# Two of four batches of the first chunk moved to the path of the later chunks, in a linear attention with a feed-forward layer behind it

## The chip, the cores and the metric

The kernel runs on one core of a Trainium2 chip. The metric is device time in microseconds (us) of one execution; lower is better. A core has five engines with a queue each: TensorE (PE in the rows; PEld is its weight load), VectorE (DVE), ScalarE (ACT), GpSimd (POOL) and SyncE (SP, which here only issues DMAs). An engine works through its queue in order and waits where an instruction's inputs are not there yet.

## The reference

Inputs `r`, `k`, `v`, `w` have the shape (4 batches, 8 heads, 768 steps, 48), `u` is (8, 48). Per batch and head a state of 48 x 48 is carried over the steps:

```python
cur   = outer(u * k_t, v_t)
y_t   = r_t @ (state + cur)
state = w_t[:, None] * state + outer(k_t, v_t)
```

The result, rearranged to 3072 tokens of 384, goes through a feed-forward layer: `h = relu(x @ w_in)` with 384 x 2048 weights, then `(h * h) @ w_out`. All is fp32 at the outside.

## The kernel before, in words

**Tiling.** The 768 steps are cut into 6 chunks of 128. A unit is one chunk of one batch (24 units). Inside a unit the recurrence becomes matrix products: a running product of `w` over the chunk (VectorE scans, line 538), keys and receptances scaled by it and its inverse (lines 545 to 566), scores, a mask, and the product with `v`; the state is carried from chunk to chunk. The `u` term stands on the diagonal of the scores: a bonus sum beta per step and head, the sum over 48 of r, u and k.

**The two paths of a unit.** Chunk 0 (there is no state yet) has a path of its own: inputs are turned by TensorE (line 521), scores (line 760), the mix with `v` (lines 784, 801), keys turned back (line 776) and state sums (line 794) are separate pieces of TensorE, with a hop to ScalarE or VectorE between them. Its bonus sums are a VectorE product (line 554), four matmuls (line 579) and a ScalarE copy (line 585). Units of chunks 1 to 5 go through a staged path instead: keys are turned (line 639), and one block of TensorE holds the mix of one unit together with the scores and state products of the next (lines 672, 681, 654, 691). Its bonus sums are two GpSimd products over the untransposed inputs (lines 588, 590), a VectorE reduction (line 593) and three small VectorE operations that move halves (lines 596 to 598). Its output is written in four banks (lines 615, 618), one of which is spread over the others by six small DMAs (line 729), and the four banks are cleared by ScalarE (line 826). In chunk 0 the output needs no such DMAs.

**The feed-forward layer.** It runs for each chunk over 16 slices f of the 2048, with fp32 values split in a leading and a remaining part. The first layer is nine matmuls (line 864), then ScalarE and VectorE make the square and its two parts (lines 869 to 876; line 876 is the last of them and is VectorE's), and the second layer is three matmuls per batch (line 882). In chunk 0 the slices f = 0 to 5 are done for batches 0 and 1 first (256 columns), and then for batches 2 and 3; from f = 6 on all four go together (512 columns). So chunk 0 has 12 half slices and 10 full ones.

**Weights.** They arrive as 16 blocks and are split once, while chunk 0 runs: a ScalarE pass (line 430), three VectorE passes (lines 434, 438, 443), a ScalarE pass (line 450) and two GpSimd subtractions of 384 columns each (line 452).

**What sets the order.** The program is a list of steps (`P.add(engine, cost, rank, function, r=..., w=...)`); the table ORDER gives the order in which they are issued, PLACES the buffer of each, and FILLS puts idle transposes (line 352) into TensorE's queue where a gap is planned. Each engine runs its steps in that order.

## Time and profile before

| | |
|---|---|
| median of 3 runs | 521.7 us (520.2 to 523.99) |
| the profiled execution | 519.77 us, its span 518.1 us |
| TensorE busy | 503.7 us, 97% of the span |
| VectorE, ScalarE, GpSimd busy | 364.5, 318.6 and 102.7 us |
| granted TensorE clock | 0.998 of 2.4 GHz over the span |
| moved by DMA | 48.73 MB |

A row of the timeline gives the start, the duration, the engine, the line, the operation and the tiles (out <- in), and in brackets the idle time before it and what ended it. Times are from the start of the span. Durations of neighbouring rows overlap a little, since an instruction starts before the one ahead of it has quite ended.

### The profile page before, as it was taken

How to read it: one execution, taken by the hardware profiler on the slowest of the kernel's cores; microseconds unless marked ns; L12 is line 12 of the kernel's file. 1: busy time of each engine (PE TensorE's matmuls, PEld its weight loads, DVE VectorE, ACT ScalarE, POOL GpSimd, SP SyncE). 2: the span in 40 equal slices, each digit the busy share in tenths (PEclk: the TensorE clock that was granted, in tenths of full speed). 3: DMA queues.
4: the chain of work that ended last, by engine and by line, in shares of the span. 5: the costliest groups of instructions: out<-in, count | busy, mean ns of one | idle time of the engine just before them, and what ended most of it. 6: DMA issues, size and time to landing. Idle time of an engine off the chain costs nothing.

```text
span 518.1 us, 13748 instructions
## 1 busy us (share of the span) xinstructions
PE 503.7 (97%) x5432; PEld 457.2 (88%) x5432; DVE 364.5 (70%) x799; ACT 318.6 (61%) x870; POOL 102.7 (20%) x157
## 2 busy tenths in 40 slices
PE   8989899998999999999999999999999999999996
PEld 7879888888999999988899889899888888998895
DVE  6999899999788888759886667678376364333232
ACT  4989889988856767667566375564544353423232
POOL 2134942646021041210402101303000000000000
PEclk9999999999999999999999999999999999999999
DMA  8999998246547565565661572771181000100001
GB/s 162 213 223 184 245 207 179 55 112 105 112 76 124 106 92 110 104 105 85 100 139 32 95 116 44 116 126 28 36 130 32 3 19 6 58 16 1 1 0 65
DMA packets 188311, 48.73 MB, mean 94 GB/s; under 512 B 178001, under 2 KB 183122, under 8 KB 188242
## 3 DMA queue, kind: packets, MB, share of 16 engines
q1 hardware_dynamic: 187664, 47.01, 47.8%
q8 instruction: 44, 0.72, 0.6%
q10 hardware_dynamic: 578, 0.79, 0.4%
q14 instruction: 25, 0.20, 0.1%
HBM read 31.66 MB, written 4.72 MB: 70 GB/s over the span
## 4 chain that ended last, share of the span: by engine, by line
PE 79%; DVE 8%; ACT 4%; DMA 4%; issue 2%; SPq 2%; POOL 0%; ACTq 0%; DVEq 0%; POOLq 0%
PE hp L864 34%; PE ob L882 34%; PE ob L672 2%; PE ob L691 2%; PE a L681 2%; DMA st<-in_r_dram 2%; PE a L654 1%; DMA ri<-in_moe_w_in_dram 1%; PE hp L639 1%; DVE q L438 1%; ACT m L634 1%; DVE g L876 1%; SPq L507 1%; DVE q L443 1%; DMA st<-in_k_dram 1%
## 5 line engine op out<-in xcount | busy, mean ns | idle before, releaser
L882 PE MATMUL ob<-wo,g 128*128 128x384 f32 x1152 | 226.7, 339 | 1.4 <-DVE g L876 1.4
L864 PE MATMUL hp<-x,wi 128*128 128x512 f32 (+1 forms) x1062 | 221.9, 354 | 2.4 <-DVE g L876 2.0
L882 PEld LDWEIGHTS ob<-wo,g 128*128 128x128 f32 x1152 | 199.6, 188 | 9.5 <-DVE g L876 1.7
L864 PEld LDWEIGHTS hp<-x,wi 128*128 128x128 f32 x1062 | 174.5, 188 | 28.6 <-DVE g L876 3.5
L869 ACT ACTIVATE t<-hp 128x512 f32<-128x512 f32 (+1 forms) x118 | 60.9, 518 | 81.1 <-PE hp L864 47.1
L873 DVE SCALAR_TENSOR_TENSOR hp<-hp,t 128x512 f32<-128x512 f32 (+1 forms) x96 | 58.1, 606 | 69.3 <-ACT t L869 68.9
L876 DVE TENSOR_TENSOR g<-hp,g 128x512 fp32r<-128x512 f32 (+1 forms) x118 | 69.1, 587 | 39.6 <-ACT g L875 38.7
L875 ACT CAST g<-hp 128x512 fp32r<-128x512 f32 (+1 forms) x118 | 59.5, 505 | 43.0 <-DVE hp L873 42.4
L662 POOL MEMSET S<- 1x1 f32 x20 | 1.8, 88 | 237.3 <-PE ob L672 237.2
L634 ACT ACTIVATE m<-diag,beta 128x64 f32<-128x64 f32 x160 | 40.4, 337 | 1.2 <-DVE beta L597 1.1
L618 DVE SCALAR_TENSOR_TENSOR x<-ob,x 112x128 fp32r<-112x128 f32 x80 | 21.3, 284 | 17.9 <-ACT x L615 14.8
L826 ACT COPY ob<-zero 112x128 f32<-112x128 f32 x80 | 20.7, 268 | 19.4 <-DVE x L618 10.0
L615 ACT ACTIVATE x<-ob 112x128 fp32r<-112x128 f32 x80 | 19.2, 278 | 18.4 <-PE ob L691 14.8
L452 POOL TENSOR_TENSOR wi<-q,wi 128x384 fp32r<-128x384 f32 x16 | 20.8, 1320 | 37.7 <-ACT wi L450 37.7
L538 DVE TENSOR_TENSOR_SCAN pt<-pt,zero 112x128 f32<-112x128 f32 x64 | 24.5, 421 | 3.7 <-DMA pt<-st 2.4
L588 POOL TENSOR_TENSOR st<-st 128x384 f32<-128x384 f32 x20 | 21.0, 1050 | 26.6 <-DMA v<-in_v_dram 15.9
L590 POOL TENSOR_TENSOR st<-st,un 128x384 f32<-128x384 f32 x20 | 23.1, 1160 | 1.0
L452 POOL TENSOR_TENSOR wo<-q,wo 128x384 fp32r<-128x384 f32 x16 | 17.0, 1080 | 30.5 <-ACT wo L450 30.5
L483 DVE STREAM_TRANSPOSE st<-st 128x1152 f32<-128x1152 f32 x16 | 21.5, 1359 | 0.3 <-ACT st L609 0.3
L562 DVE TENSOR_TENSOR pt<-pt,m 112x512 f32<-112x512 f32 x24 | 18.9, 787 | 0.5 <-ACT Ec L561 0.2
L556 DVE TENSOR_TENSOR pt<-pt 112x508 f32<-112x508 f32 x24 | 18.5, 770 | 0.1
L563 DVE SCALAR_TENSOR_TENSOR m<-pt,m 112x512 f32<-112x512 f32 x24 | 17.8, 742 | 0.3
(121 smaller groups left out, 541.0 us busy)
## 6 DMA issues: line engine op xcount, KB each, us to landing
pt<-st SPq DMA_DIRECT2D x96, 96.0 KB, 3.1
ro<-in_moe_w_out_dram SPq DMA_DIRECT2D x8, 768.0 KB, 7.7
v<-in_v_dram SPq DMA_DIRECT2D x96, 48.0 KB, 3.1
out_dram<-q SPq DMA_DIRECT2D x20, 192.0 KB, 2.1
ri<-in_moe_w_in_dram SPq DMA_DIRECT2D x32, 96.0 KB, 5.1
ri<-in_moe_w_in_dram SPq DMA_DIRECT2D x8, 384.0 KB, 6.2
st<-in_k_dram SPq DMA_DIRECT2D x8, 384.0 KB, 4.6
st<-in_w_dram SPq DMA_DIRECT2D x8, 384.0 KB
```

What stands on the lines that cost most here:

```text
L452: P.add("pool", 1.0, rank(8 * k + 5), lambda q=q, tt=tt, z=z: G.tensor_tensor(out=tt[:, 1, z * 384:z * 384 + 384], in0=q.tile[:, z * 384:z ...
L483: V.transpose(out=zt[:, i].rearrange("a t p q i -> a t (p q) i"), in_=sv[:, :, i].rearrange("s t p q x -> s t (p q) x"))
L538: lambda p=p: V.tensor_tensor_scan(out=pt[:, 0, p], data0=src(0)[:, p], data1=zero.broadcast_to([HP, C]), initial=1.0, op0=ALU.mult, op1=A ...
L590: P.add("pool", 0.97, rank("ru"), lambda: G.tensor_tensor(out=rk(), in0=rk(), in1=un.rearrange("s (h d) -> s h d", d=D), op=ALU.mult), r=[ ...
L618: made.append(P.add("dve", c2, rank(nm + "l"), lambda y=y, hi=hi, lo=lo: V.scalar_tensor_tensor(out=lo(), in0=y(), scalar=-1.0, in1=hi().b ...
L634: A.activation(M.tile[:, o:o + Q], diag2, AF.Copy, scale=beta.tile[:, i:i + 1])
L864: T.matmul(hp.tile[:, 0:n], wi[f][:, wl, kt], xT[:, kt, xl, xs], start=(m == 0), stop=(m == 3 * KT - 1))
L869: P.add("act", 0.49 if full else 0.28, rank("g1"), lambda: A.activation(t(), h(), AF.Relu), r=[hp], w=[(g, 1)])
L873: P.add("dve", 0.605 if full else 0.337, rank("g2"), lambda: V.scalar_tensor_tensor(out=h(), in0=h(), scalar=0.0, in1=t(), op0=ALU.max, op ...
L875: P.add("act", 0.48 if full else 0.26, rank("g3"), lambda: A.copy(out=hi(), in_=h()), r=[hp], w=[(g, 0)])
L876: P.add("dve", 0.605 if full else 0.335, rank("g4"), lambda: V.tensor_tensor(out=lo(), in0=h(), in1=hi().bitcast(F32), op=ALU.subtract), r ...
L882: T.matmul(obs[b][:, 0:DM], g.tile[0][:, gl, o:o + C], wo[f][:, wl], start=(f == 0 and m == 0), stop=(f == NF - 1 and m == 2))
```

## The change

Batches 2 and 3 of chunk 0 take the staged path of the later chunks: a new flag `first` (chunk 0 and batch below 2) stands where `c == 0` stood, so the old path serves batches 0 and 1 alone. The two units become the first two stages, their bonus sums go to GpSimd and VectorE, and their outputs go through the four banks, the six DMAs and the clearing. The two GpSimd subtractions per weight block become one of 768 columns. The tables ORDER, PLACES and FILLS are new throughout (they are left out below). No other arithmetic changes.

```diff
-            for z in range(2):
-                P.add("pool", 1.0, rank(8 * k + 5), lambda ...: G.tensor_tensor(out=tt[:, 1, z * 384:z * 384 + 384], ..., op=ALU.subtract),
-                      r=[q, lead], w=[(nm, g, "rest", z)])
+            P.add("pool", 1.9, rank(8 * k + 5), lambda q=q, tt=tt: G.tensor_tensor(out=tt[:, 1], in0=q.tile, in1=tt[:, 0].bitcast(F32), op=ALU.subtract),
+                  r=[q, lead], w=[(nm, g, "rest")])
...
+        first = c == 0 and b < 2
...
-        vt = Slot("v", 4 * c + b) if c else Slot("v0")
+        vt = Slot("v0") if first else Slot("v", 4 * c + b)
...
-            home = (["o0", "o1", "o2"], ["o3", "hp", "hp"], ["o0", "o1", "o2"], ["o3", "a", "o2"])[b] if c == 0 else ["hp"] * 3
+            home = (["o0", "o1", "o2"], ["o3", "hp", "hp"])[b] if first else ["o2", "o3", "hp"] if (c, b) == (0, 2) else ["hp"] * 3
...
-                if c and i in COPIED:
+                if not first and i in COPIED:
...
-        summed = c == 0
+        summed = first
...
-        if c:
+        if not first:
             M, Kt, kp = Ms[0], Slot("m", unit), Slot("hp")
...
-            if (c, b) == (1, 0):
+            if (c, b) == (0, 2):
                 clear(rank)
...
     for i in range(2 * B):
         attention(i // B, i % B, lambda nm, i=i: RANKS.unit(i // B, i % B, nm))
+        if i in (2, 3):
+            advance(stages[0] if i == 3 else None, stages[i - 2])
+        if i == 3:
+            advance(stages[1], None)
...
-            a, z = (stages[k] if 0 <= k < len(stages) else None for k in (i - B - 1, i - B))
+            a, z = (stages[k] if 0 <= k < len(stages) else None for k in (i - 3 if i > B else -1, i - 2))
             advance(a, z)
```

How the tables move the work is seen at three places. The first is VectorE, just ahead of the last write of batch 1's input to the feed-forward layer (line 618 on x0; pt0 holds batches 0 and 1 of chunk 0, pt1 batches 2 and 3, q0 and q1 weights that are being split). Before:

```order
L443 SCALAR_TENSOR_TENSOR q0_155<-ri0_56,q0_155 128x768
L554 TENSOR_TENSOR m2_164<-pt1_136,ob2_149 112x2x4x64
L556 TENSOR_TENSOR pt1_136<-pt1_136 112x4x127
L538 SCALAR_TENSOR_TENSOR pt1_136<-ob3_150,zero_126 112x128
L562 TENSOR_TENSOR pt1_136<-pt1_136,m4_166 112x512
L563 SCALAR_TENSOR_TENSOR m4_166<-pt1_136,m4_166 112x512
L538 SCALAR_TENSOR_TENSOR pt1_136<-ob3_150,zero_126 112x128
L618 SCALAR_TENSOR_TENSOR x0_142<-a0_153,x0_142 128x128
L618 SCALAR_TENSOR_TENSOR x0_142<-a1_154,x0_142 128x2x128
```

And with the change:

```order
L434 TENSOR_SCALAR q1_156<-q1_156 128x768
L593 TENSOR_REDUCE beta3_179<-st01_144 128x8
L438 SCALAR_TENSOR_TENSOR q1_156<-ri0_56,q1_156 128x768
L562 TENSOR_TENSOR pt1_136<-pt1_136,m5_167 112x512
L443 SCALAR_TENSOR_TENSOR q1_156<-ri0_56,q1_156 128x768
L563 SCALAR_TENSOR_TENSOR m5_167<-pt1_136,m5_167 112x512
L434 TENSOR_SCALAR q0_155<-q0_155 128x768
L566 TENSOR_TENSOR pt1_136<-pt1_136,m5_167 112x2x4x64
L618 SCALAR_TENSOR_TENSOR x0_142<-a1_154,x0_142 128x2x128
L618 SCALAR_TENSOR_TENSOR x0_142<-a0_153,x0_142 128x128
```

Batches 2 and 3 are now worked off further before batch 1's output, their reductions (line 593) among it, and the first weight block of the first layer (ri0) is split later.

The second place is TensorE, around the first first-layer product (line 864). Before:

```order
L579 MATMUL ob0_147<-ut_235,m2_164 128x4 x4
L352 MATMUL ob1_148<-ident_116 128x128 x13
L794 MATMUL a1_154<-v01_92,m0_162 64x48
...
L864 MATMUL hp1_152<-x0_142,wi0_57 128x256 x9
L521 MATMUL a1_154<-ident_116,st01_144 112x128 x4
L352 MATMUL ob0_147<-ident_116 128x128 x12
L760 MATMUL a0_153<-pt1_136 64x128
```

And with the change:

```order
L639 MATMUL hp1_152<-ident_116,pt1_136 128x112 x4
L352 MATMUL ob3_150<-ident_116 128x128 x12
L639 MATMUL hp0_151<-ident_116,pt1_136 128x112 x4
L794 MATMUL a1_154<-v01_92,m3_165 64x48
...
L864 MATMUL hp1_152<-x0_142,wi0_57 128x256 x9
L352 MATMUL ob3_150<-ident_116 128x128 x12
L521 MATMUL hp0_151<-ident_116,st00_143 112x128 x4
L681 MATMUL a0_153<-pt1_136 64x64 x2
```

The keys of batches 2 and 3 are turned (line 639) before the first product of the feed-forward layer, and behind it come the scores of the staged path (line 681) where those of the old path (line 760) stood.

The third place is GpSimd's queue from the end of its set-up on (st01 holds batches 2 and 3 of chunk 0, st00 batches of chunk 1 here). Before:

```order
L452 TENSOR_TENSOR wi0_57<-q0_155,wi0_57 128x384 x2
L394 TENSOR_SCALAR un_133<-un_133 128x384
L452 TENSOR_TENSOR wo0_59<-q1_156,wo0_59 128x384 x2
L452 TENSOR_TENSOR wi1_61<-q0_155,wi1_61 128x384 x2
L452 TENSOR_TENSOR wi2_65<-q1_156,wi2_65 128x384 x2
L452 TENSOR_TENSOR wo1_63<-q0_155,wo1_63 128x384 x2
L588 TENSOR_TENSOR st00_143<-st00_143 128x384
```

And with the change:

```order
L588 TENSOR_TENSOR st01_144<-st01_144 128x384
L394 TENSOR_SCALAR un_133<-un_133 128x384
L590 TENSOR_TENSOR st01_144<-st01_144,un_133 128x384
L588 TENSOR_TENSOR st01_144<-st01_144 128x384
L590 TENSOR_TENSOR st01_144<-st01_144,un_133 128x384
L451 TENSOR_TENSOR wo1_63<-q0_155,wo1_63 128x768
L451 TENSOR_TENSOR wi0_57<-q1_156,wi0_57 128x768
L451 TENSOR_TENSOR wo0_59<-q0_155,wo0_59 128x768
L451 TENSOR_TENSOR wi1_61<-q1_156,wi1_61 128x768
```

The four bonus products of batches 2 and 3 stand ahead of the first weight block, and the first block to be split belongs to the second layer.

## Rows read from the trace of the kernel before

**Rows 1.** The page, part 1: busy us of each engine, share, instructions.

```profile
PE 503.7 (97%) x5432; PEld 457.2 (88%) x5432; DVE 364.5 (70%) x799; ACT 318.6 (61%) x870; POOL 102.7 (20%) x157
```

**Rows 2.** Busy time by stretch: engines in order, then granted clock, DMA share, GB/s.

```profile
76.71:127.43 50.72, 48.30 (x543) 42.01 (x543) 47.96 (x91) 45.38 (x110) 25.34 (x29) 1.00 0.54 112
127.43:518.10 390.67, 385.43 (x4084) 351.55 (x4083) 248.25 (x572) 210.67 (x597) 44.71 (x86) 1.00 0.38 70
```

**Rows 3.** Waits of TensorE up to 130 us: total, times, longest.

```profile
PE hp L864 <- DVE g L876: 2.0, 3, 1.0
PE ob L882 <- DVE g L876: 1.4, 1, 1.4
```

**Rows 4.** Timeline, the first 512-column product of the first layer.

```profile
76.71 2.38 PE L864 MATMUL hp<-x,wi 128*128 128x512 f32 x9 [1.04 <-DVE g L876]
```

**Rows 5.** Busy time by stretch, 7.45 to 76.65 us cut in three: the last, the sum.

```profile
53.36:76.65 23.29, 20.78 (x159) 18.81 (x157) 21.79 (x30) 19.38 (x45) 16.16 (x13) 1.00 1.05 226
sum 69.20, PE 64.14 PEld 57.79 DVE 65.16 ACT 60.69 POOL 29.69; mean PE 21.38 PEld 19.26 DVE 21.72 ACT 20.23 POOL 9.90
```

**Rows 6.** TensorE alone: batch 2's pieces on the old path, four stretches summed.

```profile
sum 4.96, PE 4.96; mean PE 1.24
```

**Rows 7.** TensorE alone: a unit on the staged path, two stretches.

```profile
131.11:131.43 0.32, 0.32 (x6) 1.00 0.05 10
135.87:137.89 2.02, 2.02 (x129) 1.00 0.10 33
```

**Rows 8.** TensorE alone: a stretch that holds one turning of four (line 521).

```profile
32.90:33.30 0.40, 0.40 (x10) 1.00 1.11 230
```

**Rows 9.** Timeline of TensorE: the first turning, a run of idle transposes.

```profile
5.07 1.06 PE L521 MATMUL ob<-ident,st 128*112 128x128 f32 x4
...
25.55 1.62 PE L352 MATMUL ob<-ident 128*128 128x128 f32 x13
```

**Rows 10.** Timeline of VectorE: first scans, a weight pass, the twelfth line 876.

```profile
7.45 1.37 DVE L538 TENSOR_TENSOR_SCAN pt<-ob,zero 112x128 f32<-112x128 f32 x4 [3.43 <-PE ob L521]
48.93 0.95 DVE L443 SCALAR_TENSOR_TENSOR q<-ro,q 128x768 uint32<-128x768 uint32 x1
76.24 0.41 DVE L876 TENSOR_TENSOR g<-hp,g 128x256 fp32r<-128x256 f32 x1
```

**Rows 11.** Groups by line and form: count, busy us, mean ns, idle before.

```profile
L538 DVE TENSOR_TENSOR_SCAN pt<-ob,zero 112x128 f32<-112x128 f32 x16 | 6.1, 409 | 3.4 <-PE ob L521 3.4
L593 DVE TENSOR_REDUCE beta<-st 128x8 f32<-128x384 f32 x20 | 10.9, 543 | 0.0
L713 DVE COPY_PREDICATED m<-caus,a 128x256 f32<-128x256 uint8 x40 | 17.2, 437 | 0.1
L701 DVE TENSOR_TENSOR S<-a,S 112x96 f32<-112x96 f32 x40 | 9.7, 246 | 3.5 <-PE a L654 3.5
L763 DVE COPY_PREDICATED m<-caus,a 128x384 f32<-128x384 uint8 x6 | 3.3, 581 | 1.4 <-ACT hp L871 0.9 <-PE a L760 0.5
L554 DVE TENSOR_TENSOR m<-pt,ob 112x512 f32<-112x512 f32 x3 | 2.0, 683 | 0.2 <-ACT pt L548 0.2
L618 DVE SCALAR_TENSOR_TENSOR x<-ob,x 112x128 fp32r<-112x128 f32 x80 | 21.3, 284 | 17.9 <-ACT x L615 14.8 <-PE ob L882 2.5
```

**Rows 12.** Timeline of VectorE, beside GpSimd's work and (last row) without it.

```profile
53.28 1.17 DVE L556 TENSOR_TENSOR pt<-pt 112x508 f32<-112x508 f32 x1
74.67 1.65 DVE L443 SCALAR_TENSOR_TENSOR q<-ro,q 128x768 uint32<-128x768 uint32 x1
77.43 0.88 DVE L596 TENSOR_TENSOR beta<-beta 64x4 f32<-64x4 f32 x1
80.27 0.16 DVE L596 TENSOR_TENSOR beta<-beta 64x4 f32<-64x4 f32 x1
```

**Rows 13.** Groups by line and form: the first GpSimd product of a staged unit.

```profile
L588 POOL TENSOR_TENSOR st<-st 128x384 f32<-128x384 f32 x20 | 21.0, 1050 | 26.6 <-DMA v<-in_v_dram 15.9 <-DVE st L483 10.1 <-PE hp L521 0.4
```

**Rows 14.** DMA issues: count, KB of each, median us to landing.

```profile
x<-x SPq DMA_DIRECT2D x60, 32.0 KB, 2.0
```

More of the change, by code (lines that the diff above doesn't have):

```diff
@@ L450, in split_w @@
             P.add("act", 0.73, rank(8 * k + 4), lambda q=q, tt=tt: A.copy(out=tt[:, 0], in_=q.tile), r=[q], w=parts + [lead])
-            for z in range(2):
-                P.add("pool", 1.0, rank(8 * k + 5), lambda q=q, tt=tt, z=z: G.tensor_tensor(out=tt[:, 1, z * 384:z * 384 + 384], in0=q.tile[:, z * 384:z * 384 + 384], in1=tt[:, 0, z * 384:z * 384 + 384].bitcast(F32), op=ALU.subtract),
-                      r=[q, lead], w=[(nm, g, "rest", z)])
+            P.add("pool", 1.9, rank(8 * k + 5), lambda q=q, tt=tt: G.tensor_tensor(out=tt[:, 1], in0=q.tile, in1=tt[:, 0].bitcast(F32), op=ALU.subtract),
+                  r=[q, lead], w=[(nm, g, "rest")])
     both = {}
@@ L502, in attention @@
         vals = lambda i: st.tile.rearrange("s (t b x) -> s t b x", t=3, b=2)[:, i, ui, front:].rearrange("s (h d) -> s h d", h=H)
-        vt = Slot("v", 4 * c + b) if c else Slot("v0")
-        vo = lambda p, j, y: PC + (4 * y + p % 2 * 2 + j) * (D if c else J)
+        vt = Slot("v0") if first else Slot("v", 4 * c + b)
+        vo = lambda p, j, y: PC + (4 * y + p % 2 * 2 + j) * (J if first else D)
         VK = [(vt, q, y) for q in range(2) for y in range(2)]
@@ L507, in attention @@
             P.add("sp", 0.32, rank("v"), lambda q=q, y=y: nc.sync.dma_start(
-                out=(vt.tile[:, PC:].rearrange("s (y h d) -> s y h d", y=2, d=D) if c else vt.tile.rearrange("s (y h d) -> s y h d", y=2, d=J)[:, :, :, PC:J])[q * Q:q * Q + Q, y],
+                out=(vt.tile.rearrange("s (y h d) -> s y h d", y=2, d=J)[:, :, :, PC:J] if first else vt.tile[:, PC:].rearrange("s (y h d) -> s y h d", y=2, d=D))[q * Q:q * Q + Q, y],
                 in_=v[b, q * 4:q * 4 + 4, c * C + y * Q:c * C + y * Q + Q].rearrange("h s d -> s h d")), w=[(vt, q, y)], runs=4 * Q, issue=0.66)
         if c < 2:
-            home = (["o0", "o1", "o2"], ["o3", "hp", "hp"], ["o0", "o1", "o2"], ["o3", "a", "o2"])[b] if c == 0 else ["hp"] * 3
+            home = (["o0", "o1", "o2"], ["o3", "hp", "hp"])[b] if first else ["o2", "o3", "hp"] if (c, b) == (0, 2) else ["hp"] * 3
             ps = {}
@@ L527, in tl @@
                 return x.tile if type(x) is Slot else obs[x[1]]
-            inner = lambda t: c == 1 and t in COPIED
+            inner = lambda t: not first and t in COPIED
             src = lambda t: pt[:, t] if inner(t) else tl(ps[t]).rearrange("a (p s) -> a p s", p=NP)[0:HP]
@@ L546, in attention @@
         P.add("act", 0.535, rank("exp"), lambda: A.activation(yv(), yv(), AF.Exp, scale=-1.0), w=[y0])
-        if c == 0:
+        if first:
             P.add("act", 0.49, rank("rc"), lambda: A.activation(flat(pt[:, 1]), flat(src(1)), AF.Copy, scale=one_sided), r=keys(1), w=[PT[1], PT[1] + (0,), ("turned", b)])
-        Ms = [Slot("m", unit) for j in range(1 if c else 2)]
+        Ms = [Slot("m", unit) for j in range(2 if first else 1)]
         turned = lambda x: flat(x).rearrange("a (q g t) -> a q g t", q=2, g=4)
         flat = lambda x: x.rearrange("a p s -> a (p s)")
-        summed = c == 0
+        summed = first
         if summed:
@@ L556, in attention @@
         P.add("dve", 0.595, rank("rt"), lambda: V.tensor_tensor(out=pt[:, 1, :, 1:C], in0=pt[:, 1, :, 1:C], in1=pt[:, 0, :, 0:C - 1], op=ALU.mult),
-              r=EK + (keys(1) if c else []), w=[PT[1], ("turned", b)], port=True)
-        RK = [PT[1]] + ([PT[1] + (0,)] if c == 0 else [])
+              r=EK + ([] if first else keys(1)), w=[PT[1], ("turned", b)], port=True)
+        RK = [PT[1]] + ([PT[1] + (0,)] if first else [])
         Ec = Slot("Ec")
@@ L848, in xkeys @@
             return [("xT", c)]
-        return [("xT", c % 2, b, n, h) for n in range(2 if c == 0 else KT) for h in ("hi", "lo")] + [("xT", c % 2, b, j, q) for j in range(2) for q in range(KT)]
+        return [("xT", c % 2, b, n, h) for n in range(2 if c == 0 and b < 2 else KT) for h in ("hi", "lo")] + [("xT", c % 2, b, j, q) for j in range(2) for q in range(KT)]
     SLOW = -1
@@ L857, in ffn @@
         hp, g = Slot("hp"), Slot("g")
-        wkeys = lambda nm: [(nm, f // 2, "lead"), (nm, f // 2, "rest", 0), (nm, f // 2, "rest", 1)]
+        wkeys = lambda nm: [(nm, f // 2, "lead"), (nm, f // 2, "rest")]
         def first():
```

4 lines of the change are left out of this document (2 added, 2 removed), and 204 rows, old and new, of tables (ORDER, PLACES).

## The prediction

> **What bounds the kernel now.** I read the page's busy times first, then busy time by stretch, TensorE's waits, and the timeline around the longest of them. TensorE is busy 97% of the span and no other engine over 70% [rows 1], and from 127.43 us on it is busy 385.4 of 390.7 us [rows 2]: whatever TensorE need not do is worth its full length there. But the change touches only the start. There VectorE holds the pace: up to 130 us the waits that cost TensorE most end with VectorE's line 876 [rows 3], the last step before the second layer. The last of them ahead of a first-layer product is 1.04 us, for the product that starts at 76.71 [rows 4]; it is the thirteenth first-layer product of chunk 0, the first with 512 columns, and what it waited for is the twelfth line 876, at 76.24 [rows 10]. Between its first scan at 7.45 [rows 10] and that instruction's end, VectorE is busy 65.2 of 69.2 us and ScalarE 60.7 [rows 5]. After 76.71 TensorE is busy 48.3 of 50.7 us [rows 2], with one wait of 1.4 [rows 3].
>
> So I cut the program at the thirteenth first-layer product. The order of both programs shows that from there TensorE has the same instructions left, counted by line, but for three turnings of four (line 521), which the change has already done. At 0.40 us each [rows 8] that is **-1.2 us**. All idle transposes lie ahead of the cut in both. The rest is one question: when does the thirteenth product start?
>
> **TensorE's own account up to the cut.** For each of the two batches the old path's pieces go: scores (32.07 to 32.90), bonus matmuls and the first part of the mix (34.73 to 36.19), the rest of the mix and the keys (37.15 to 39.21), the state sums (42.61 to 43.22), together 4.96 us [rows 6]. The staged path puts 0.32 for the keys and 2.02 for the block in their place [rows 7]. That is 2 x (4.96 - 2.34) = 5.2 us less. Three turnings of four come ahead of the cut, +1.2, and 11 idle transposes, 91 for 80, at 1.62 / 13 = 0.12 us [rows 9], +1.4. TensorE alone would reach the cut 2.6 us earlier, and with the -1.2 behind it the kernel would gain 3.8. This is a saving on an engine that waits there, so it is not the forecast.
>
> **VectorE's account up to the cut.** I counted its instructions in the order from the first scan to the twelfth line 876, 112 before and 139 now. Added: four scans (1.4, from the first row of [rows 10]); one more each of lines 556, 562 and 563, all 112 x 512 like line 554, 0.68 each, 2.0; two reductions at 0.54, 1.1; twelve operations that move halves, at 0.16 free of GpSimd [rows 12], 1.9; eight writes of x out of four banks at 0.284, 2.3; eight state sums (701, 704) at 0.246, 2.0; four masks at 0.437, 1.7 [all rows 11]. Gone: two weight passes at 0.95 [rows 10], 1.9; two products (554) at 0.683, 1.4; four masks (763) at 0.581, 2.3; four writes of x of the old kind and two state sums, which I price as the new ones of their kind, 1.1 + 0.5 [rows 11]. Added 12.4, gone 7.2: +5.2. Neighbours overlap: the four scans take 1.37 us in a row [rows 10] where four times the line's 0.409 [rows 11] is 1.64, so about 0.08 for each of the 15 instructions that are more and aren't the small chained ones, -1.2. Together **+4.0 us**. About 2 of these 4 are work of chunk 1 done earlier, but TensorE doesn't get that back, since behind the cut it is TensorE that sets the pace.
>
> **Start.** The first turning in TensorE's queue is now that of `w` for the scans, behind the 16 idle transposes; before, it stood behind another turning and two idle transposes. The turning that stood first was done at 6.13 [rows 9], the first scan began at 7.45 [rows 10]. I take **-1.3 us**; the bounds are 0 (the data are late) and -1.3.
>
> **GpSimd beside VectorE.** Ahead of the cut GpSimd has two more of line 588, at 1.05 [rows 13], two of its companion line 590 on the same columns, which I price alike, and two state products (708) on half the columns, which I price at half: 2 x 2.6 = 5.2 us more. Some VectorE instructions grow while GpSimd works: a weight pass takes 1.65 for 0.95, a move of halves 0.88 for 0.16 [rows 12, 10]. From 53.28 to 74.67 there are ten such rows, of which the first and the last are shown, and they sum to 6.3 us over what the same lines take alone, beside 16.2 us of GpSimd [rows 5]. So a microsecond of GpSimd cost VectorE 0.39 there; in the two stretches before, GpSimd was less busy. At 0.39 it is **+2.0 us**; the bounds are 0 and 5.2 (every microsecond, as the 0.88 for 0.16 would have it). The single subtraction of 768 columns for two of 384 I cost at nothing: the same columns, half as many chances to block, each twice as long.
>
> The Trainium skill, "SBUF — State Buffer", section "SBUF: two separate sides", speaks against this part: the port pair that VectorE and GpSimd share is "an exclusive lock", held for the whole instruction. The row of 0.88 us for 0.16 agrees with it. By that rule alone an operation could wait out a whole subtraction of 768 columns, and the added 5.2 us would count in full, 3.2 us more than in my sum.
>
> **Waits of VectorE.** It idles 69.2 - 65.2 = 4.0 us [rows 5]. The new order begins with twelve scans in a row, of three batches instead of one, and puts work of batches 2 and 3, which waits for nothing else, between the hops of batches 0 and 1. I take half, **-2.0 us**, with bounds -4.0 and +4.0 (as much again, since ScalarE, busy 60.7 of the 69.2, has its own eight clearings and eight bank copies more).
>
> **Sum.** -1.3 + 4.0 + 2.0 - 2.0 = +2.7 to the cut, -1.2 behind it: +1.5. TensorE's later waits (the 1.4 of [rows 3]) I leave as they are, bounds -1.4 and +1.4. On the profiled execution's 519.77 us this gives 521.3. Its time lies 1.9 below the median of the runs shown, so the same shift from the median would give 523.2; I say **521.5**, near the lower, since the lowest of the three runs lies there too. A change of under 1%, 5.2 us, is no change for this measurement.
>
> **Rivals.**
> - *TensorE sets the pace after all.* If the new order takes all of VectorE's 4.0 us of idle time away and GpSimd costs little, the sum above falls to -1.3 + 4.0 + 0 - 4.0 - 1.2 = -2.5; and if VectorE's early work on chunk 1 lets the waits of 2.0 and 1.4 us [rows 3] go too, to -5.9. By TensorE's account alone it is -3.8, with these waits -7.2. For it: the first stretch mixes more independent work. Against it: VectorE's 94% busy leaves little. Time 513 to 518, middle 516. Chance 0.3, of which 0.18 is over 1%.
> - *GpSimd holds VectorE up, slower than before.* The four bonus products now stand ahead of all weight blocks in GpSimd's queue, beside VectorE instructions that read and write SBUF, and their reductions stand in VectorE's queue ahead of the first weights' passes. If each added microsecond of GpSimd costs VectorE one and no wait goes, it is -1.3 + 4.0 + 5.2 - 1.2 = +6.7, 526.5 to 528.5. It passes 1% from 0.71 us per microsecond on. For it: [rows 12]. Against: the rate of 0.39. Chance 0.2, three quarters of it over 1%.
> - *The small DMAs make TensorE wait.* Batches 2 and 3 now reach the feed-forward layer through six DMAs of 2.0 us to landing [rows 14]. If they are issued some 0.6 us apart, the last lands 5 to 6 us after the last write of x. TensorE has four turnings (1.6 us) and fifteen second-layer products there, about 4 us, to cover them. 1 to 5 us on top of the sum: 522 to 526. Chance 0.1.
> - That the first product starts later is sure (batch 1's x has 15 more VectorE instructions net ahead of it, among them four weight passes and two reductions) and is no rival by itself: VectorE's account contains it.
>
> **How the numbers follow.** The forecast has 0.4, and nearly all of it lies within 1%. Faster by over 1%: 0.18 of the first rival and a little of the forecast, 0.2. Slower by over 1%: 0.15 of the second, 0.03 of the third, a little of the forecast, 0.2. Within: 0.6. The rivals reach from 512.6 (TensorE's account without waits) to 528.5, and with all bounds at once it would be 534; the range that leaves out 2 in 10 is 515 to 528.
>
> **What would show it.** In the new trace: the first line 876 some 5 to 8 us later than 35 us, the twelfth at 76 to 81 us, and the thirteenth first-layer product right behind it. If that product starts before 75 us, VectorE's account was too dear; if after 82, look for VectorE rows stretched beside lines 588, 590 and 451, or for TensorE waiting on x from the DMAs ahead of the seventh first-layer product. Behind the cut TensorE should be as full as before; waits there of more than 3 us in total would make the cut the wrong place to count.

## The result and the profile after

The changed kernel takes **529.5 us** (median of four runs, 526.6 to 531.2) where the kernel before takes 522.4 (four runs): 1.0147 times as long, interval 1.0113 to 1.018. The forecast of 521.5 and its range to 528 lie below. The profiled execution took 528.3 us, its span is 526.6; against the 519.77 and 518.1 of before that is +8.5. A single kernel's runs differ by 4 to 5 us here, so all ratios below are of medians.

The page of the changed kernel, part 1 and the row of TensorE's granted clock:

```profile
PE 503.5 (96%) x5479; PEld 457.3 (87%) x5479; DVE 365.8 (69%) x813; ACT 319.8 (61%) x876; POOL 105.8 (20%) x151
PEclk9889989999999999999999999999999999999999
```

TensorE has 47 instructions more and the same busy time as before [rows 1], though it has less to do: part of its work ran at half speed. The clock row has an 8 in its second, third and sixth slice; before, all 40 digits were 9. The same in numbers, TensorE by stretches of 5 us (busy time, instructions, granted clock, DMA share, GB/s), after:

```profile
15.00:20.00 5.00, 3.36 (x52) 0.90 1.19 247
20.00:25.00 5.00, 5.00 (x81) 0.76 1.18 184
25.00:30.00 5.00, 2.15 (x51) 0.93 1.03 262
30.00:35.00 5.00, 5.00 (x55) 0.73 0.93 161
...
70.00:75.00 5.00, 5.00 (x25) 0.66 1.20 218
```

All of these are 1.00 in the kernel before. Cut finer, they are three stretches at 1.2 GHz (0.50): 19.0 to 22.4, 29.2 to 32.7 and 70.2 to 73.6 us. At half speed for these 10.3 us TensorE falls back by at most 5.1. Ahead of each it had waited for VectorE. The waits up to 130 us after (total, times, longest), for [rows 3]:

```profile
PE hp L864 <- DVE g L876: 3.4, 2, 2.2
PE a L784 <- DVE m L763: 1.7, 1, 1.7
PE a L760 <- DVE pt L566: 1.6, 1, 1.6
...
PE ob L882 <- ACT ob L826: 1.5, 1, 1.5
PE a L794 <- DVE x L618: 1.1, 1, 1.1
```

The first two dips stand behind the waits for lines 566 and 763, the third behind the 2.2 us of line 876.

**Where the first-layer products stand.** First the kernel before, TensorE's timeline, a row that is not shown above:

```profile
71.10 3.50 PE L864 MATMUL hp<-x,wi 128*128 128x256 f32 x18
```

These are 18 matmuls, two products in one row, and 3.50 us is one of 256 columns (1.24) and one of 512 (2.26). So the thirteenth product began in this row, and the one at 76.71 [rows 4] is the **fourteenth**, and the second with 512 columns. The same stretch after:

```profile
68.90 1.34 PE L864 MATMUL hp<-x,wi 128*128 128x256 f32 x9 [2.21 <-DVE g L876]
70.08 1.03 PE L882 MATMUL ob<-wo,g 128*128 128x384 f32 x3
71.00 2.29 PE L864 MATMUL hp<-x,wi 128*128 128x256 f32 x9
73.09 2.00 PE L882 MATMUL ob<-wo,g 128*128 128x384 f32 x9
74.93 1.24 PE L864 MATMUL hp<-x,wi 128*128 128x256 f32 x9
...
79.21 2.25 PE L864 MATMUL hp<-x,wi 128*128 128x512 f32 x9
81.31 2.27 PE L882 MATMUL ob<-wo,g 128*128 128x384 f32 x12
83.42 2.26 PE L864 MATMUL hp<-x,wi 128*128 128x512 f32 x9
```

and of VectorE the twelfth line 876, for the last of [rows 10]:

```profile
79.71 0.42 DVE L876 TENSOR_TENSOR g<-hp,g 128x256 fp32r<-128x256 f32 x1
```

The fourteenth product starts at 83.42, 6.7 us later than before. The twelfth line 876 is only 3.5 later (76.24 to 79.71). The product waits for nothing: since 70.08 TensorE has no gap. It is the engine that is late, by the 2.21 us at 68.90 and by rows at half speed (2.29 us for 1.24 at 71.00).

**The sum of the profiled runs.** Twelfth line 876, +3.5. TensorE behind it, +3.2. From the fourteenth product on there is less work left than before, by the order and the steady durations -2.25: three turnings of four (1.2), and six second-layer matmuls (1.05) that now stand ahead of that product. Yet from there to the last turning of keys (line 639, at 435.65, before at 428.03) it takes 352.2 us where it took 351.3, so +3.2 is lost on the way. The tail adds 0.9, all of it behind TensorE's last matmul. Together 8.5.

**Where half of the 3.2 goes** is seen around 109 to 117 us after, GpSimd, VectorE, ScalarE and TensorE:

```profile
108.88 1.84 POOL L451 TENSOR_TENSOR wi<-q,wi 128x768 fp32r<-128x768 f32 x1 [0.77 <-ACT wi L450]
112.48 1.84 POOL L451 TENSOR_TENSOR wo<-q,wo 128x768 fp32r<-128x768 f32 x1 [1.76 <-ACT wo L450]
```

```profile
109.16 2.37 DVE L443 SCALAR_TENSOR_TENSOR q<-ro,q 128x768 uint32<-128x768 uint32 x1
...
112.69 2.17 DVE L556 TENSOR_TENSOR pt<-pt 112x508 f32<-112x508 f32 x1
...
115.62 1.10 DVE L618 SCALAR_TENSOR_TENSOR x<-ob,x 112x128 fp32r<-112x128 f32 x4
```

```profile
115.93 0.27 ACT L826 COPY ob<-zero 112x128 f32<-112x128 f32 x1 [2.56 <-DVE x L618]
...
116.62 0.79 PE L882 MATMUL ob<-wo,g 128*128 128x384 f32 x3 [1.53 <-ACT ob L826]
```

Both VectorE instructions start 0.2 to 0.3 us behind one of GpSimd's and end when that one's end plus their own length has passed: 108.88 + 1.84 + 0.95 [rows 10] = 111.67, measured 111.53; 112.48 + 1.84 + 0.68 [rows 11] = 115.00, measured 114.86 (line 556 works on the shape of line 554). So they stood still until the subtraction had ended. The write of x behind them is late, so the clearing of the bank, and TensorE waits 1.53 us. Two more such cases lie at 81.52 (line 563, 2.34 for 0.68) and 128.76 us (line 597, 1.77 for 0.16). Not every instruction is held: line 876 took its usual 0.68 us at 86.08 beside the subtraction of 85.68, and beside those of 95.36 and 98.15, when VectorE was at lines 483, 701, 713 and 876, no row is longer than elsewhere. The waits of TensorE behind the fourteenth product (83.4 to 230 us) after:

```profile
PE hp L864 <- DVE g L876: 2.1, 2, 1.1
PE ob L882 <- ACT ob L826: 1.5, 1, 1.5
PE hp L864 <- ACT m L641: 1.5, 1, 1.5
PE ob L691 <- issue: 0.7, 1, 0.7
PE hp L864 <- DVE pt L538: 0.2, 1, 0.2
```

They are 6.0 us; before, from 76.7 on, 3.6, of which 1.04 is the fourteenth product's own [rows 4]. One of them has nothing to do with the start. It lies in the next chunk, TensorE and ScalarE:

```profile
187.31 1.33 PE L864 MATMUL hp<-x,wi 128*128 128x256 f32 x9 [1.52 <-ACT m L641]
...
186.14 0.48 ACT L891 COPY q<-ob 128x384 f32<-128x384 f32 x1 [1.84 <-DVE x L618]
186.52 0.27 ACT L826 COPY ob<-zero 112x128 f32<-112x128 f32 x1
186.72 0.54 ACT L641 COPY m<-hp 128x448 f32<-128x448 f32 x1
```

ScalarE stands 1.84 us for a write of x on VectorE, and its copy of keys (line 641) behind that is late. The kernel before has no such wait, and no GpSimd subtraction is left at that time: this is the new order of the steps. The same 1.5 us stand in the traces of e1_split, e3_nobonus, e10_four, e12_nosums, e16_four_fills and e18_all_three, and no run below tries to take them away.

### The profile page after: what moved, and what is told of

Same layout as the page of the kernel before. It is cut to its first block, busy times and chain, and to the rows that moved or that the text cites. A ratio compares the mean times of both kernels' runs of the same rounds, so it can differ in the third digit from the quotient of the medians.

```text
span 526.6 us, 13867 instructions
## 1 busy us (share of the span) xinstructions
PE 503.5 (96%) x5479; PEld 457.3 (87%) x5479; DVE 365.8 (69%) x813; ACT 319.8 (61%) x876; POOL 105.8 (20%) x151
## 4 chain that ended last, share of the span: by engine, by line
PE 80%; DMA 6%; DVE 6%; ACT 3%; SPq 2%; issue 1%; POOL 0%; DVEq 0%; POOLq 0%; ACTq 0%
PE ob L882 35%; PE hp L864 35%; DMA ro<-in_moe_w_out_dram 3%; PE ob L672 2%; DMA ri<-in_moe_w_in_dram 2%; PE ob L691 2%; PE a L681 2%; PE a L654 1%; PE hp L639 1%; DMA st<-in_r_dram 1%; DVE q L443 1%; SPq L417 1%; DVE g L876 1%; DVE q L438 1%; PE a L352 1%
## 5 line engine op out<-in xcount | busy, mean ns | idle before, releaser
L634 ACT ACTIVATE m<-diag,beta 128x64 f32<-128x64 f32 x176 | 44.4, 341 | 1.1 <-DVE beta L597 1.1
L618 DVE SCALAR_TENSOR_TENSOR x<-ob,x 112x128 fp32r<-112x128 f32 x88 | 23.1, 283 | 22.2 <-ACT x L615 19.4
L588 POOL TENSOR_TENSOR st<-st 128x384 f32<-128x384 f32 x22 | 27.0, 1229 | 36.4 <-DMA st<-in_k_dram 15.0
L615 ACT ACTIVATE x<-ob 112x128 fp32r<-112x128 f32 x88 | 21.8, 280 | 20.3 <-PE ob L691 16.0
L826 ACT COPY ob<-zero 112x128 f32<-112x128 f32 x88 | 23.0, 270 | 18.1 <-DVE x L618 10.6
L538 DVE TENSOR_TENSOR_SCAN pt<-pt,zero 112x128 f32<-112x128 f32 x64 | 26.6, 449 | 1.5 <-DMA out_dram<-q 0.5
L713 DVE COPY_PREDICATED m<-caus,a 128x256 f32<-128x256 uint8 x44 | 19.0, 438 | 3.6 <-PE a L654 2.7
L451 POOL TENSOR_TENSOR wi<-q,wi 128x768 fp32r<-128x768 f32 x8 | 15.5, 1933 | 28.0 <-ACT wi L450 28.0
L563 DVE SCALAR_TENSOR_TENSOR m<-pt,m 112x512 f32<-112x512 f32 x24 | 19.8, 830 | 0.2
L562 DVE TENSOR_TENSOR pt<-pt,m 112x512 f32<-112x512 f32 x24 | 17.3, 720 | 3.6 <-ACT m L546 2.7
```

The lines of the kernel that those rows point to most:

```text
L538: lambda p=p: V.tensor_tensor_scan(out=pt[:, 0, p], data0=src(0)[:, p], data1=zero.broadcast_to([HP, C]), initial=1.0, op0=ALU.mult, op1=A ...
L588: P.add("pool", 0.97, rank("rk"), lambda: G.tensor_tensor(out=rk(), in0=rk(), in1=vals(2), op=ALU.mult), r=[(st, ui, 2)], w=[(st, ui, 1)])
L618: made.append(P.add("dve", c2, rank(nm + "l"), lambda y=y, hi=hi, lo=lo: V.scalar_tensor_tensor(out=lo(), in0=y(), scalar=-1.0, in1=hi().b ...
L634: A.activation(M.tile[:, o:o + Q], diag2, AF.Copy, scale=beta.tile[:, i:i + 1])
L826: P.add("act", 0.16, rank("zero"), lambda p=p: A.copy(out=obs[p][0:HP, DM:], in_=zero[0:HP].broadcast_to([HP, C])), w=[("YO", p)], after=t ...
```

## The experiments

Three suspects follow from the two traces: the long subtraction, which makes VectorE stand still; the four bonus products on GpSimd and their sums; and the start, where the first product is 9.4 us later (29.05 to 38.42) and TensorE's clock falls. All ratios are to the kernel before, on the same chip; the chips differ from run to run, and the kernel before takes 521.1 to 522.6 us on them. By their two intervals the difference of two versions is uncertain by some 0.4%, 2 us; what is smaller is a hint and not shown.

**The subtraction: cut in the changed kernel, joined in the kernel before.**

```diff
 # e1_split: the changed kernel
-lambda ...: G.tensor_tensor(out=tt[:, 1], ...)
+lambda ...: [G.tensor_tensor(out=tt[:, 1, z*384:z*384+384], ...) for z in range(2)]
 # e2_join: the kernel before
-lambda ..., z=z: G.tensor_tensor(out=tt[:, 1, z*384:z*384+384], ...)
+lambda ..., z=z: z or G.tensor_tensor(out=tt[:, 1], ...)
```

> The changed kernel with GpSimd's subtraction of 768 columns issued as two of 384 again, everything else in the same order. Theory H (hold): a VectorE instruction that runs beside the subtraction lasts as long as the subtraction, so the single one costs the later stalls: the 1.53 us ahead of the second-layer product at 116.62, the 1.14 at 86.81 and the 0.95 at 132.14 go or shrink, and some 1 us at the start; the kernel gains 3 to 5 us, 524.5 to 526.5. No VectorE row of line 443, 556, 563 or 566 is longer than 1.7 us. Theory S (start): the loss arises ahead of the first first-layer product (38.42 us, before 29.05), because the first block of w_out is loaded and split ahead of the first block of w_in, and work of batches 2 and 3 stands ahead of batch 1's; the split subtraction gives at most 1 us, 528.5 to 530. Theory C (clock): TensorE at its lower clock after its waits is what costs; 528.5 to 530 here.

> The kernel before with GpSimd's two subtractions of 384 columns joined to one of 768, everything else in the same order. Theory H: slower by 2 to 5 us, 524.5 to 527.5, with VectorE rows of more than 2 us for 0.68 or 0.95 in the first 130 us. Theories S and C: the start is as before, so no change, 522 to 523.5.

Cut in two, the changed kernel takes 527.0 us, 1.0094 (1.0064 to 1.0124), 2.5 us less. The kernel before with one long subtraction takes 523.9, 1.0044 (1.0021 to 1.0068), 2.3 more. Both lie between what theory H and the others had forecast. Two programs of quite different order give about the same price; in the kernel before it is shown clear of noise. It is the length that counts, not GpSimd's time: of the first 200 us, GpSimd's subtractions of the first layer's weights before and with the long one:

```profile
L452 POOL TENSOR_TENSOR wi<-q,wi 128x384 fp32r<-128x384 f32 x16 | 20.8, 1320 | 37.7 <-ACT wi L450 37.7
```

```profile
L452 POOL TENSOR_TENSOR wi<-q,wi 128x768 fp32r<-128x768 f32 x8 | 17.0, 2120 | 40.7 <-ACT wi L450 29.3 <-DMA v<-in_v_dram 11.3
```

Joined they keep GpSimd busy for less, 17.0 against 20.8 us, and the kernel is slower. In the changed kernel with the cut, VectorE's two instructions of above:

```profile
111.57 1.54 DVE L443 SCALAR_TENSOR_TENSOR q<-ro,q 128x768 uint32<-128x768 uint32 x1
...
114.27 1.52 DVE L556 TENSOR_TENSOR pt<-pt 112x508 f32<-112x508 f32 x1
```

They are 0.8 and 0.65 us shorter, and from the fourteenth product to the last turning of keys it takes 349.9 us for 352.2: of the 3.2 lost there, 2.4 come back. That run's first product is at 42.26, though, and its fourteenth at 86.55: the start is worse than in the profiled run after, so part of the gain hides (it is the slowest of its five runs).

**Cut again, in four.**

```diff
 # e9_four_before: the kernel before; e10_four: the changed kernel, range(4) of 192
-lambda ..., z=z: G.tensor_tensor(out=tt[:, 1, z*384:z*384+384], ...)
+lambda ..., z=z: [G.tensor_tensor(out=tt[:, 1, o:o+192], ...) for o in (z*384, z*384+192)]
```

> The kernel before with each of GpSimd's subtractions of 384 columns in two of 192, nothing else changed. Theory H (VectorE waits for the whole GpSimd instruction that it meets, so its length is the price): joining the pieces cost 2.3 us, halving them gives back half of that again, 0.5 to 1.5 us: 520 to 521.2; no VectorE row of line 434, 438 or 443 is more than 0.6 us longer than alone beside line 452. Theory N (there is no more to win below 384 columns, the number of meetings doubles as the length halves): 521 to 522.5.

> The changed kernel with the subtraction in four of 192 columns. Two of 384 gave 527.0. Theory H: 0.5 to 1.5 us more, 525.5 to 526.5. Theory N: 526.5 to 527.5.

The kernel before goes to **519.05 us, 0.9956** (0.9931 to 0.998; ten runs). It beats both kernels. The changed one goes to 525.0, 1.0066 (1.004 to 1.0091). Of the same place VectorE's timeline in the kernel before and cut in four (the before row behind this one is the 1.65 of [rows 12]):

```profile
73.03 1.60 DVE L438 SCALAR_TENSOR_TENSOR q<-ro,q 128x768 uint32<-128x768 uint32 x1
```

```profile
72.86 0.95 DVE L438 SCALAR_TENSOR_TENSOR q<-ro,q 128x768 uint32<-128x768 uint32 x1
73.84 1.25 DVE L443 SCALAR_TENSOR_TENSOR q<-ro,q 128x768 uint32<-128x768 uint32 x1
```

The stretch goes from 1.35 us in the pair to 0.3. The bonus products cut in halves as well:

```diff
 # e15_all_small: e9_four_before, lines 588 and 590
-lambda: G.tensor_tensor(out=rk(), ...)
+lambda: [G.tensor_tensor(out=rk()[:, o:o+4], ...) for o in (0, 4)]
```

> The kernel before with GpSimd's subtractions in pieces of 192 columns (alone 519.05) and its bonus products (lines 588 and 590, 384 columns) in two halves each as well. Theory H: 0.3 to 1 us more than the first alone, 518 to 518.8, 0.992 to 0.995 of the kernel before. Theory N: 519 to 519.5, the products meet VectorE too seldom, or the added fixed part of each instruction takes the gain.

520.0 us, 0.9976 (0.9956 to 0.9997): no further gain, as far as these intervals tell. It fits the theory that nothing is left to take, by which what there was to win lay beside the weight passes.

**The bonus products and sums.** Left out in these are the products of lines 588 and 590 for batches 2 and 3 of chunk 0, in e12_nosums their reductions and halves too (beta is a constant).

```diff
 # e3_nobonus: the changed kernel; e11_split_nobonus: e1_split with the same
-lambda: G.tensor_tensor(out=rk(), ...)
+lambda: c == 0 or G.tensor_tensor(out=rk(), ...)
 # e12_nosums: e11_split_nobonus and
-lambda: V.tensor_reduce(out=beta.tile[:, 0:H], ...)
+lambda: V.memset(beta.tile, 0.01) if c == 0 else V.tensor_reduce(...)
-halves
+(lambda: None) if c == 0 else halves
```

> The changed kernel without the four bonus products of batches 2 and 3 in chunk 0 on GpSimd (lines 588 and 590, five busy us ahead of 30 us; the bonus term of these batches is then not the reference's), their place in VectorE's order and everything else kept. Theory G (the second rival of the prediction: GpSimd's added products hold VectorE up): VectorE's rows beside them shrink (line 563 twice in 2.40 us at 14.76 to 1.3) and the kernel gains 1.5 to 4 us, 525.5 to 528. Theory O (the order of the work ahead of the first first-layer product, and not GpSimd's added products, is what costs): the rows shrink as well, but the gain of 1 us at 15 us ends in a later wait of the same chain: 528.5 to 530.

> The changed kernel with the subtraction in two of 384 columns and without GpSimd's four bonus products of batches 2 and 3 (their bonus term is then not the reference's). Alone the one gave 527.0, the other 526.7, against 529.5. If the two prices are separate (the bonus products cost at the start, the long subtraction behind it) they add up: 523.5 to 525. If both are the same stall seen twice: 526 to 527.

> As the run before it, and without VectorE's share of the same bonus either: in chunk 0 the two reductions (line 593) and the six moves of halves (lines 596 to 598) of batches 2 and 3 are left out, a fill of the sums with a constant stands in their place (1.1 + 1.0 us of VectorE less). If VectorE paces the program there, the 2 us come back whole: 521.5 to 523. If TensorE does (it was 3.3 us behind VectorE at the fourteenth first-layer product), little does: 523.5 to 525.

526.7 us, 1.0096 (1.0073 to 1.012), without the products: 2.8 less. But in its profiled run the first product still comes at 37.80. The clock is at 1.00 from 15 to 25 us there, and at 0.65 and 0.67 in the two stretches of 5 us behind, so this run does not tell whether the clock makes it late; e18_all_three below does. And of the 1.8 us that the fourteenth is earlier, 1.2 come between the tenth and the eleventh, since the clock does not fall there. With the cut the products seem to be worth less: 525.7, 1.0083 (1.0051 to 1.0115), 1.3 under the cut alone. If the two prices added up it would be 1.0043, just below that interval. That both buy off the same standing still fits, but is not shown. Without the sums as well, 524.4, 1.0066 (1.004 to 1.0091); in the profiled run (the fastest of its ten) the stretch behind the fourteenth product is as long as before for its work, though the 1.5 us of line 641 are in it, and still the kernel is slower than before. That rest lies at the start: its fourteenth product comes 4.1 us later than before.

**Idle transposes and the clock.**

```diff
 # e5_fills: the changed kernel, FILLS with 48 idle transposes more
+37: (12, 'a', 0), 49: (8, 'ob', 0), 81: (12, 'ob', 1), 543: (16, 'side', 3),
 # e8_lessfill: e1_split, FILLS with 14 fewer
-83: (12, 'ob', 2), 126: (12, 'ob', 3),
+83: (5, 'ob', 2), 126: (5, 'ob', 3),
```

> The changed kernel with 48 more idle transposes placed into four waits of TensorE: 12 ahead of batch 0's scores (wait of 1.64 us at 17.82), 8 ahead of its state sum (1.15 at 26.83), 12 ahead of batch 1's mix (1.70 at 29.39) and 16 ahead of the ninth first-layer product (2.21 at 68.90). Theory C: TensorE's granted clock stays at 2.4 GHz in 15 to 35 us and in 70 to 75 us, where it was 0.66 to 0.93 of it; the two first-layer products and nine second-layer matmuls at half speed behind 69 us give back 1.7 us and the start up to 1: 526.5 to 528. Theories H and S: 529 to 530.5, the idle transposes take only waits.

> The changed kernel with the subtraction in two pieces (as in the run with that alone, 527.0) and 5 instead of 12 idle transposes at each of two places ahead of the first first-layer product (ahead of the second part of batch 1's mix, where 12 took 2.24 us at the lower clock, and ahead of batch 1's state sum). Theory F (idle transposes in TensorE's queue, at half speed behind a wait, hold batch 1's chain up): the first product 0.5 to 2 us sooner and 525 to 526.3 in all. Theory O: what batch 1's chain waits for there is VectorE and ScalarE; 526.5 to 527.5.

With 48 more: 530.1 us, 1.0148 (1.01 to 1.0197), no change. The clock stays at 1.00 from 70 to 75 us and TensorE's way from the ninth product to the fourteenth shrinks by some 1.2 (13.3 us for 14.5), but the clock falls at 17 to 21 and 34 to 38 all the same. With 14 fewer: 529.3, 1.0144 (1.0118 to 1.017), 2.2 **slower** than e1_split (the two intervals just overlap), which neither theory had. The one by which idle transposes only stand in TensorE's way falls; from 30 to 35 us the profiled run, the slowest of its four, is wholly at half speed:

```profile
30.00:35.00 5.00, 4.64 (x30) 0.50 1.20 193
```

Next they were tried on the versions cut in four, and the other way round on the kernel before:

```diff
 # e16_four_fills: e10_four, 35 more
+37: (8, 'a', 0), 49: (5, 'ob', 0), 81: (8, 'ob', 1), 543: (14, 'side', 3),
 # e17_less_before: the kernel before, 14 fewer
-90: (13, 'ob', 1), 125: (12, 'ob', 0),
+90: (6, 'ob', 1), 125: (5, 'ob', 0),
```

> The changed kernel with the subtraction in four pieces (525.0, median clock 0.988) and 35 more idle transposes, fewer than the waits hold: 8 in the wait of 1.64 us ahead of batch 0's scores, 5 in that of 1.15 ahead of its state sum, 8 in that of 1.70 ahead of batch 1's mix, 14 in that of 2.21 ahead of the ninth first-layer product. Theory C (the clock is a cause): where the median clock rises, the time falls by 0.35 us per 0.001; with 0.994, 523; if the clock stays at 0.988 the run tells nothing. Theory W (the waits are the cause and the clock goes with them): 524.5 to 526 whatever the clock.

> The kernel before with 6 instead of 13 idle transposes ahead of batch 1's state sum (25.55 us) and 5 instead of 12 ahead of batch 2's scores (30.8 us). They fill time in which TensorE has nothing to do, and nothing else is changed. Theory C: TensorE falls to its lower clock behind them for one stretch of 3 to 4 us or more, the median clock to 0.993 or less, and the kernel is 1.5 to 3 us slower, 522.7 to 524. Theory W: no wait is added, so 520.8 to 522.

35 more bring the changed kernel to 523.3 us, 1.003 (0.9998 to 1.0062), and the median granted clock of its runs from 0.988 to 0.9955: 1.7 us less, which is under the uncertainty. 14 fewer in the kernel before take its clock from 0.998 to 0.9935 and cost nothing that can be seen: 521.4, 0.9992 (0.9959 to 1.0025). That a fall of the clock has its price where TensorE is behind, and none where it would wait anyway, fits both; it is not shown, since the transposes left out could have given back what the clock took. The version that is fastest of all has a dip of its own:

```profile
35.00:40.00 5.00, 4.49 (x41) 0.66 1.15 272
```

All three remedies in one (e16_four_fills without bonus products and sums of batches 2 and 3):

> The run before last (subtraction in four pieces, 35 more idle transposes) without the bonus sums of batches 2 and 3 in chunk 0: GpSimd's four products, VectorE's two reductions and six moves of halves are left out and a constant stands for the sums. Theory V (these sums on VectorE and GpSimd take what TensorE is spared): faster than the kernel before at last, 518 to 520.5. Theory R (the rest is the order ahead of the first products, which starts them 8 us later): 521 to 523, as the sums left out gave only 1.3 us more than GpSimd's part alone in the earlier pair.

521.4 us, 0.9983 (0.9959 to 1.0007): level with the kernel before. By the ratios the sums were worth 2.5 us here, in the pair of e11_split_nobonus and e12_nosums 0.9. TensorE up to the first product, and that product:

```profile
0.00:36.81 36.81, 32.11 (x405) 1.00 0.99 201
...
36.81 1.34 PE L864 MATMUL hp<-x,wi 128*128 128x256 f32 x9
```

It comes 7.8 us later than before with the clock at 1.00 throughout, without the bonus sums, and with the subtraction in four. So these three account for some 1.6 of the 9.4 us; the rest is the order of the start, its idle transposes with it, or the path itself. The fourteenth comes at 81.83, 5.1 later than before, so what TensorE saves is used up at the start.

**The order of the start.** In e4_hoist 120 steps that the first product needs are issued ahead of 70 others; in e13_order (from e1_split) and e14_order_before (from the kernel before) the first 560 steps are rearranged by the same rule; in e6_moved and e7_moved_before, the first 620 of the two kernels, loads among them. (e6_moved and e13_order have the subtraction in two as well, e6_moved also the 14 idle transposes fewer.)

```diff
 # e4_hoist, e13_order, e14_order_before, e6_moved, e7_moved_before
-ORDER = [...]
+ORDER = [...]   # the same steps, the first ones in another order
```

> The changed kernel with the 120 steps that the first first-layer product needs moved ahead of the 70 others that stood among them (in their old order, the loads of w_in ahead of those of w_out too); nothing behind that product is moved. Theory S: the first product starts at 30 to 34 us instead of 38.4 and about half of what it gains is kept to the end, since batches 2 and 3 then come later: 525 to 527.5. Theory H: 528.5 to 531, since the later stalls remain. Theory C: no clear gain, 528 to 531.

> The changed kernel with the subtraction in two of 384 columns and with its first 560 steps in another order: batch 1's products, masks and rows of x ahead of batch 3's sums and of batch 2's scans and reductions on VectorE, its copies and keys (lines 805 and 809) ahead of work of batch 2 on ScalarE, its loads and the loads of v sooner; no step is added or left out and the idle transposes stay. The same order as the changed kernel gave 527.0. Theory O (the order ahead of the first first-layer product): that product starts 2 to 5 us sooner than in that kernel's profile (42.3) and the kernel takes 520 to 524. Theory P (the path costs VectorE and ScalarE more than TensorE saves, in any order): 525.5 to 528.

> The kernel before with its first 560 steps rearranged in the same manner, nothing else changed: the control. By theory O what is gained in the run above is particular to the changed kernel's order: here 520 to 522. If moves of this kind are worth 2 us or more here as well (under 519.5), the gain of the run above says nothing on the change.

> The changed kernel with the subtraction in two pieces, the two groups of 12 idle transposes cut to 5, and the first 620 of its 2474 steps in another order: each engine's queue has the same steps, most within ten places of where they stood (batch 1's first mask and its rows of x go ahead of work of batches 2 and 3 on VectorE, batch 1's keys and receptance are loaded sooner). Theory O: the path with 3.8 us less work for TensorE is sound and the loss sits in the order; with batch 1's chain ahead the first product starts at 34 to 37 us and the kernel takes 518 to 523. Theory P (the staged path costs VectorE and ScalarE more ahead of the first products than TensorE saves, in any order): no better than 525.

> The kernel before with its first 620 steps rearranged by the same kind of local moves, nothing else changed: a control for the run above. If such moves alone are worth 2 us or more here too (under 520), a better time of the run above says little on the path; if this is 521 to 524, it does.

e4_hoist: 539.7 us, 1.0393 (1.0321 to 1.0465). The first product does come early, the second 20 us behind it (line 864 has the number 877 in this kernel, whose tables are longer):

```profile
33.13 1.34 PE L877 MATMUL hp<-x,wi 128*128 128x256 f32 x9 [1.11 <-ACT m L654]
...
53.87 1.34 PE L877 MATMUL hp<-x,wi 128*128 128x256 f32 x9
```

The theory that the first product's lateness alone is the loss falls in this form. e13_order 530.7, 1.0182 (1.0153 to 1.0211), e14_order_before 531.2, 1.0177 (1.0133 to 1.0221): both slower than any theory had forecast, and the old path in the foreign order ends level with the new one, slower than its own by about as much as the change costs. So an order alone can cost that much. In e14_order_before the clock is at 0.50 from 11 to 28 us, so this pair does not tell the order from the path. e6_moved and e7_moved_before, 1.1031 (1.1002 to 1.106) and 1.1115 (1.108 to 1.1149), say nothing on either. A load of v was moved ahead in SyncE's queue and waited for its buffer there, and all loads behind it with it; in the kernel before the longest such wait is 11.9 us (the queue's waits in e6_moved: total, times, longest):

```profile
SPq L507 <- PE ob L691: 78.1, 6, 36.2
```

## Why the prediction was wrong

**What the forecast missed.** Its sum was 521.3, the profiled run took 528.3. Of the 7.0 between them, 0.8 arise up to the twelfth line 876, 2.2 between it and the fourteenth product (the 3.2 of above less the 1.05 of matmuls moved ahead), 3.2 from there to the last turning of keys and 0.9 in the tail (all rounded).

**The step that failed first: "The single subtraction of 768 columns for two of 384 I cost at nothing: the same columns, half as many chances to block, each twice as long."** It measured 2.3 us (e2_join) to 2.5 (e1_split), and 2.4 of the 3.2 behind the fourteenth product came back with the cut. Twice as long is not outweighed by half as often. An instruction that is held by a subtraction stands still for what is left of it, so the wait grows with the length; and VectorE is busy enough there that most subtractions find one to hold. The chain of line 443, 556, 618, 826 and 882 carries this to TensorE. The Trainium skill, "SBUF — State Buffer", section "SBUF: two separate sides", holds that the port pair is held for the whole instruction; the trace agrees (2.37 us for 0.95, ended 0.14 ahead of the sum of both). The prediction weighed that rule against the 0.39 per microsecond that it had taken from rows with 384 columns, a rate that was measured at that length only.

**The cut was read wrongly,** and behind it TensorE's path. "It is the thirteenth first-layer product": it is the fourteenth, since a row with x18 holds two. More than a name hangs on it: the step "when does the thirteenth product start?" was answered by VectorE's account alone, with TensorE "right behind". In truth TensorE was behind: the fourteenth product started 3.7 us after the twelfth line 876, where before it was 0.5.

**TensorE's clock was in no term.** The trace of before shows 1.00 in every stretch, and the sum took TensorE's durations from it. But the new order makes TensorE wait for VectorE at 17.8, 29.4 and 68.9 us, and behind each it ran at half speed. How much of the 7 us this is, is not settled; what TensorE lost directly is at most the 5.1 of above in the profiled run. e16_four_fills gives back some 1.7 us with the clock partly restored; over 62 runs of the kernel before, the time falls by 0.35 us for each 0.001 of mean clock (correlation -0.74), which for 0.998 to 0.986 would be 4, but a correlation does not tell whether the clock or the waits ahead of its falls are the cause; in e17_less_before a lower clock came with no loss.

**VectorE's account came out near by luck.** Forecast +2.7 to the twelfth line 876, measured +3.5; the place, 76 to 81 us, is met with 79.71. But its terms are not met. All engines from the first scan to the end of that instruction (busy time of TensorE, its weight load, VectorE, ScalarE, GpSimd), for the sum of [rows 5], and the largest of VectorE's waits in it (total, times, longest):

```profile
5.86:80.13 74.27, 64.75 (x835) 58.87 (x834) 65.68 (x140) 64.05 (x176) 31.30 (x24) 0.93 0.98 204
...
DVE g L876 <- ACT g L875: 3.2, 3, 1.6
```

VectorE is busy 65.7 us for 65.2: its work, forecast +4.0 for the instructions and +2.0 for GpSimd, grew by 0.5. It idles 8.6 us for 4.0: its waits, forecast -2.0 with a bound of +4.0, grew by 4.6. The start gave -1.6 for -1.3. GpSimd was busy only 1.6 us more, not 5.2. So "I take half, **-2.0 us**" had the wrong sign: the new order gave VectorE more to wait for, at line 876 on ScalarE above all. Two errors of 5.5 and 6.6 us cancelled.

**What held.** The first line 876 at 41.88 is 6.8 later, forecast 5 to 8. The row that was to show a wrong cut did so: waits behind it over 3 us, measured 6.0.

**The work saved on TensorE** was put at 3.8 us, and rightly as far as e18_all_three tells: with the clock at 1.00 up to the first products TensorE is busy 503.7 us there, as before, with 35 idle transposes more, an estimated 4.2 us at 0.12 each [rows 9]. But the saving never shows as time: it is spent at the start.

**The rivals.** The one that ends slower (GpSimd holds VectorE up, 526.5 to 528.5) came nearest; its mechanism is right, but it named the four added products alone (2.8 us by e3_nobonus, 1.3 beside the cut) and not the length of the subtraction (2.3 to 2.5). That TensorE sets the pace, to the kernel's gain, fell. The small DMAs cost nothing: TensorE runs into the seventh product (63.77) without a wait.

**Open** stays how much of the late start belongs to the order found for this path and how much to the path itself, what the falls of the clock cost, and what the 1.5 us at 187.31 would be worth.

## What to carry to other kernels

Price a long GpSimd instruction beside busy VectorE by its length and not by its share: cut it (768 columns in four pieces were worth 4.5 us in one kernel here, 4.8 from joined in the other), also where GpSimd itself gets slower by it. Before a sum is cut at an instruction, count its rows by shape, for one row may hold two; and where a change makes TensorE wait in places where it did not, write its clock into the sum as a term. A sum that comes out near does not prove its terms: look each of them up in the new trace. A load that is moved ahead in a queue takes all loads behind it with it, so look first at when its buffer comes free.

## What the runs showed of the hardware that was not expected

- GpSimd's rows stretch too: 768 columns took 1.84 us at 108.88, 2.30 at 81.01, where a VectorE row of line 438 (80.66, 0.95 us) was still running when it started. Of the first layer's weights 768 columns cost GpSimd 3.6 us in four pieces (895 ns each), 2.6 in two (1320), 2.1 in one (2120), and the kernel's time goes the other way.
- The granted clock was 1.00 or 0.50 in every short stretch looked at, and a few instructions that do no work move it: 14 idle transposes fewer took the median clock of the kernel before from 0.998 to 0.9935 (e17_less_before), at no loss that can be seen; in the changed kernel 14 fewer came with 2.2 us more (e8_lessfill).
- In e6_moved, 10% slower than the kernel before, one load waited 36.2 us for its buffer in SyncE's queue, where the longest such wait of the kernel before is 11.9.
